# Strided and local attention with a hard-swish feed-forward on one core: where the first two batches' probabilities are turned, and how TensorE is kept busy before its first product

## The chip, the cores and the metric

The kernel runs on one core of a Trainium2 chip. A core has five instruction streams that matter here: TensorE (PE in the profile), VectorE (DVE), ScalarE (ACT), GpSimd (POOL), and SyncE (SP), which issues the DMAs. Each stream runs in its program order; a semaphore makes an instruction wait for another stream or a DMA. The metric is device microseconds from start to end, the median of several runs.

## The reference

Eight batches, eight heads, 576 positions of 64. In heads 0 to 3 a query sees itself and the 31 positions before it; in heads 4 to 7 it sees earlier positions whose number leaves the same rest by 32. The result, reordered to 4608 tokens of 512, goes through a feed-forward layer of width 2048. Weights are in float64, q, k and v in float32.

```python
scores = scale * np.matmul(q, k.transpose(0, 1, 3, 2))
rel = pos[:, None] - pos[None, :]
mask_local = (rel >= 0) & (rel < stride)                       # heads 0..3, stride 32
mask_strided = (rel >= 0) & (pos[None, :] % stride == pos[:, None] % stride)
attn = softmax(np.where(masks, scores, -1e9)); x = attn @ v    # x: [4608, 512]
h = x @ w_in                                                   # w_in [512, 2048]
g = h * np.clip(h + 3.0, 0.0, 6.0) / 6.0
out = g @ w_out                                                # w_out [2048, 512]
```

## The kernel before

**One list of operations, one planner.** The kernel writes down all its work with `op(engine, cost, function, reads, writes, due)`. `Plan.emit` (line 93) then walks a clock of its own: at each step it takes the operation that can start first on some engine (of several, the one with the smallest due time), and the order so found becomes each engine's program order. An operation may name several engines with a cost for each; the planner then also picks the engine. Due times hang on `T0`, the planned start of the first feed-forward product, and on the start of each later tile. Costs and due times set only the order; on the chip semaphores set the times.

**Attention by pairs of heads.** A batch is four pairs, `pair(g)` (line 440), taken in the order of `TURNS` (0, 2, 1, 3 for batch 0); pairs 0 and 1 are local, 2 and 3 strided. A pair's steps: transposes of q and k (`qp`, `kp` on TensorE in batch 0), scores (`ps`), mask, maximum, `less` (subtract it), exponential, sum, reciprocal, `norm`; then the normalized scores `e` are turned and set out in a block matrix (`atstr` for strided pairs, `atloc` for local ones), one for each of the pair's two heads (j = 0 and 1); then the products with v (`pv`). Two score tiles, `e_130` and `e_228` in the listings, are shared by all pairs. In batches 0 and 1 `turn` does the turning and the setting out in one step: for each block of 32 rows one DVE transpose straight into its place (four of 32x256 for a strided head, line 684; six of 32x192 for a local one, line 687). From batch 2 on `flip` transposes the whole tile in place on DVE (line 690) and `spread` copies the blocks to their places on ACT (lines 697 and 700). The local pairs of batch 0 are turned on TensorE instead (`pe`, line 371).

**x in two parts.** In batches 0 and 1 `keep_x` (line 408) splits each `pv` into a rounded part (`hi`, ACT, line 426) and the rest (`lo`, DVE, line 429), because each product of the feed-forward layer is made of three TensorE products of parts: high by high, high by low, low by high (lines 856 to 858 for `ph`, 833 to 835 for `acc`). A pair has two halves, and both parts of both halves write the same two keys, so the planner puts them in one chain: hi, lo, hi, lo. The last 64 positions of a batch go to a `left` tile.

**Weights.** Float64 weights come in as pairs of integers (`rawi`, `rawo`), and five operations turn one block into two parts: two on ACT (lines 281 and 285), a join on DVE (line 289), the high part on ACT or POOL (lines 303 and 305), the low part on POOL (line 308).

**The first 60 us.** Before the first feed-forward product TensorE would stand still for stretches; where the planner's clock sees such a stretch (line 138) it fills in `idle` products of 128x384, one for each 0.64 us (line 1570), and ahead of the first of them 46 small ones. The first tile is `ffn(0)`; then come `ffn(1)`, `ffn(2)` and three tiles of two batches.

Of the kernel before, what the change touches and what calls it, by code (L numbers as in the profile page):

```python
# [31 lines left out]
AHEAD = 27.0  # L32
OPEN = 6.0
# [4 lines left out]
T0 = 44.0  # L38
# [18 lines left out]
FEW = 46  # L57


class Plan:  # L60
# [29 lines left out]
    def emit(self, idle):  # L90
# [21 lines left out]
        while done < len(ops):  # L112
# [61 lines left out]
def attention_ffn(ctx: ExitStack, tc, q, k, v, w_in, w_out, out):  # L174
# [230 lines left out]
    def x_keys(b, c):  # L405
        return [("x", b, c, i) for i in range(2)] if b < 2 else [raw_key(b, c)]

    def keep_x(nm, b, c, puts, due):
# [4 lines left out]
        for n, (bkey, what, place, size, rest) in enumerate(puts):  # L413
# [19 lines left out]
            op("ACT", 0.15 + size * (0.0019 if strided else 0.00085), hi, reads=[bkey] + (xk if rest else []), writes=kk, give=bkey if last and whole else None, due=due + n)  # L433
            if not whole:
                op("DVE", 0.15 + size * (0.002 if strided else 0.00105), lo, reads=[bkey], writes=kk, give=bkey if last else None, due=due + 0.2 + n)
# [4 lines left out]
    def pair(g):  # L440
# [237 lines left out]
        for j in range(2):  # L678
# [9 lines left out]
            if b >= 2:  # L688
# [16 lines left out]
                op("ACT", 6 * 0.31 if loc else 4 * 0.36, spread, reads=[ekeys[j]], writes=[akeys[j]], due=due - 1.9 + j)  # L705
# [31 lines left out]
        op("PE", 1.25 * slow, values, reads=[*akeys, *vkeys], writes=[*vb, *xk, lk], take=vb, due=due - 1001,  # L737
# [80 lines left out]
    def ffn(b):  # L818
        s0, puts = start[b], []
        chunk = TILE / NFC  # L820
        xk = {c: x_keys(b, c) if b < 2 else [("x", 1, c, i) for i in range(2)] for c in range(NCC)}

# [19 lines left out]
        def first_product(fc):  # L842
# [3 lines left out]
            for n_, c in enumerate(TURNS[b]):  # L846
# [12 lines left out]
                op("PE", 0.683, mm1, reads=xk[c] + wkeys, writes=[pk],  # L859
# [744 lines left out]
```

## Time and profile before

| | |
|---|---|
| median of 3 runs | 870.25 us (869.94 to 876.99) |
| the profiled execution's own time | 871.98 us |
| its span, first to last instruction | 870.2 us |
| mean granted TensorE clock | 0.993 |
| busy: PE / DVE / ACT / POOL | 847.4 / 539.0 / 558.9 / 616.6 us |
| TensorE instructions (matmuls) | 6962 |

The span is what the profile's rows add up to; the 1.8 us beside it lie outside the first and last instruction. The profiled execution took 1.7 us more than the median of the runs. A row of the timeline gives start, length, engine, line, names and the count of merged instructions, and in brackets the idle time ahead of it with what ended it; `issue` means that nothing in the profile ended it. A 128x512 row of TensorE is drawn with its whole length, but such products start some 0.23 us apart.

### The profile page before, as it was taken

How to read it: one execution, taken by the hardware profiler on the slowest of the kernel's cores; microseconds unless marked ns; L12 is line 12 of the kernel's file. 1: busy time of each engine (PE TensorE's matmuls, PEld its weight loads, DVE VectorE, ACT ScalarE, POOL GpSimd, SP SyncE). 2: the span in 40 equal slices, each digit the busy share in tenths (PEclk: the TensorE clock that was granted, in tenths of full speed). 3: DMA queues.
4: the chain of work that ended last, by engine and by line, in shares of the span. 5: the costliest groups of instructions: out<-in, count | busy, mean ns of one | idle time of the engine just before them, and what ended most of it. 6: DMA issues, size and time to landing. Idle time of an engine off the chain costs nothing.

```text
span 870.2 us, 18946 instructions
## 1 busy us (share of the span) xinstructions
PE 847.4 (97%) x6962; PEld 683.8 (79%) x6962; DVE 539.0 (62%) x898; ACT 558.9 (64%) x1246; POOL 616.6 (71%) x606
## 2 busy tenths in 40 slices
PE   8889999999999999999999999999999999999996
PEld 6667777887888788888888878788888778888884
DVE  5688878344454538454546664466767888555586
ACT  3687657678778865877677965776744645454441
POOL 4688877587547799766676994465975987767673
PEclk9999999999999999999999999999999999999998
DMA  8968723898984455898999897877666667866636
GB/s 194 330 138 233 234 41 73 210 281 245 279 234 108 128 129 141 233 266 233 269 277 289 274 301 214 237 204 189 183 202 193 185 180 222 240 202 192 183 122 145
DMA packets 323308, 179.12 MB, mean 206 GB/s; under 512 B 182864, under 2 KB 300368, under 8 KB 323216
## 3 DMA queue, kind: packets, MB, share of 16 engines
q1 hardware_dynamic: 318564, 176.27, 71.5%
q10 hardware_dynamic: 4652, 1.64, 0.9%
q8 instruction: 55, 0.90, 0.4%
q14 instruction: 37, 0.30, 0.1%
HBM read 136.97 MB, written 40.89 MB: 204 GB/s over the span
## 4 chain that ended last, share of the span: by engine, by line
PE 82%; DMA 5%; POOL 5%; DVE 4%; ACT 2%; issue 1%; SPq 0%; POOLq 0%; DVEq 0%; ACTq 0%
PE P L1129 8%; PE P L1130 8%; PE P L1131 8%; PE cP L1452 5%; PE cP L1453 5%; PE cP L1454 5%; PE acc L833 5%; PE ph L856 5%; PE ph L857 4%; PE ph L858 4%; PE acc L835 4%; PE acc L834 4%; PE acc L1214 3%; PE acc L1215 3%; PE acc L1216 3%; PE pv L399 2%
## 5 line engine op out<-in xcount | busy, mean ns | idle before, releaser
L1470 DVE SCALAR_TENSOR_TENSOR C<-cP,C 128x512 f32<-128x512 f32 x96 | 65.7, 687 | 40.4 <-PE cP L1454 39.5
L794 POOL TENSOR_TENSOR gl<-u,gh 128x512 fp32r<-128x512 f32 x48 | 65.2, 1361 | 33.3 <-ACT gh L790 17.1
L1141 DVE TENSOR_TENSOR G<-P,G 128x512 f32<-128x512 f32 x64 | 44.0, 689 | 65.6 <-PE P L1131 53.2
L1129 PE MATMUL P<-B_T,wr 128*128 128x512 f32 x192 | 76.1, 396 | 3.9 <-ACT G L1136 2.3
L833 PE MATMUL acc<-wo,gh 128*128 128x512 f32 x192 | 77.2, 402 | 0.0
L835 PE MATMUL acc<-wo,gl 128*128 128x512 f32 x192 | 75.2, 392 | 0.3 <-POOL gl L794 0.2
L834 PE MATMUL acc<-wo,gh 128*128 128x512 f32 x192 | 74.9, 390 | 0.0
L1130 PE MATMUL P<-B_T,wr 128*128 128x512 f32 x192 | 74.8, 390 | 0.0
L1131 PE MATMUL P<-B_T,wr 128*128 128x512 f32 x192 | 74.8, 390 | 0.0
L1136 ACT COPY G<-P 128x512 f32<-128x512 f32 x64 | 37.6, 587 | 52.2 <-PE P L1131 51.7
L1367 POOL TENSOR_TENSOR sp<-G,sp 128x512 fp32r<-128x512 f32 x34 | 47.6, 1411 | 24.6 <-ACT sp L1363 22.5
L665 POOL TENSOR_TENSOR e<-e,st 128x144 f32<-128x144 f32 (+1 forms) x64 | 44.9, 704 | 20.7 <-DVE st L661 15.2
L779 DVE SCALAR_TENSOR_TENSOR u<-u,ph 128x512 f32<-128x512 f32 x48 | 32.8, 684 | 38.0 <-ACT u L776 37.8
L856 PE MATMUL ph<-x,wi 128*128 128x512 f32 x128 | 52.5, 410 | 2.3 <-ACT x L426 1.2
L857 PE MATMUL ph<-x,wi 128*128 128x512 f32 x128 | 50.8, 397 | 1.4 <-DVE x L429 0.8
L700 ACT COPY atloc<-e 32x192 f32<-32x192 f32 x144 | 50.8, 353 | 1.9 <-DVE e L690 0.3
L776 ACT ACTIVATE u<-ph,three 128x512 f32<-128x512 f32 x48 | 33.0, 687 | 28.1 <-PE ph L858 27.8
L858 PE MATMUL ph<-x,wi 128*128 128x512 f32 x128 | 50.8, 397 | 0.0
L644 DVE TENSOR_REDUCE st<-e 128x8 f32<-128x144 f32 (+1 forms) x64 | 25.6, 412 | 35.8 <-POOL e L640 35.6
L1129 PE MATMUL P<-B_B,wr 128*128 128x512 f32 x120 | 47.1, 392 | 0.0
L1130 PE MATMUL P<-B_B,wr 128*128 128x512 f32 x120 | 46.8, 390 | 0.0
L1129 PEld LDWEIGHTS P<-B_T,wr 128*128 128x128 f32 x192 | 36.0, 188 | 13.7 <-ACT G L1136 3.6
(604 smaller groups left out, 2672.6 us busy)
## 6 DMA issues: line engine op xcount, KB each, us to landing
wr<-dA SPq DMA_DIRECT2D x72, 256.0 KB
or<-do SPq DMA_DIRECT2D x32, 512.0 KB
wr<-dSu SPq DMA_DIRECT2D x48, 256.0 KB
wr<-dSv SPq DMA_DIRECT2D x48, 256.0 KB
or<-do SPq DMA_DIRECT2D x48, 256.0 KB
rawi<-in_moe_w_in_dram SPq DMA_DIRECT2D x16, 512.0 KB
rawo<-in_moe_w_out_dram SPq DMA_DIRECT2D x16, 512.0 KB
do<-wo SPq DMA_DIRECT2D x16, 512.0 KB
```

Source lines behind the costliest of these rows:

```text
L700: nc.scalar.copy(at[PAD * (a + h):PAD * (a + h) + PAD, :, rows], e[rows, :, PAD * h:PAD * h + PAD])
L794: (nc.vector if tail else nc.gpsimd).tensor_tensor(out=to, in0=src(), in1=tiles[gk[0]].bitcast(F32), op=ALU.subtract)
L833: nc.tensor.matmul(acc, gh, woh, start=fc == 0, stop=False)
L834: nc.tensor.matmul(acc, gh, wol, start=False, stop=False)
L835: nc.tensor.matmul(acc, gl, woh, start=False, stop=end)
L856: nc.tensor.matmul(ph, wih, xh, start=n_ == 0, stop=False)
L857: nc.tensor.matmul(ph, wih, xl, start=False, stop=False)
L858: nc.tensor.matmul(ph, wil, xh, start=False, stop=n_ == NCC - 1)
L1129: nc.tensor.matmul(ph, wh, xh, start=fresh and k == 0, stop=False, skip_group_check=not fresh)
L1130: nc.tensor.matmul(ph, wh, xl, start=False, stop=False, skip_group_check=not fresh)
L1131: nc.tensor.matmul(ph, wl, xh, start=False, stop=k == 1, skip_group_check=not fresh)
L1470: nc.vector.scalar_tensor_tensor(out=tiles[ck], in0=tiles[bank], scalar=1.0 / 6.0, in1=tiles[ck], op0=ALU.mult, op1=ALU.add)
```

## The change

Five edits. (1) `emit` counts the first stretch of idle time from 2.6 us (`BEGIN`) and not from 0. (2) In batches 0 and 1 all pairs but the local ones of batch 0 use `flip` in place of `turn`; each block copy is an operation of its own that ACT, POOL or DVE may take. For that the zeroing of `atstr` and `atloc` gets a second key, and `values` reads a key for each block. Strided heads also get a small memset on POOL (`again`). (3) In `keep_x` the parts of a half have keys of their own: a half's lo waits for its own hi, and the second half's hi no longer waits for the first half's lo; the products read all these keys. (4) The copies to `left` get a due time 3 us later. (5) `T0` goes from 44 to 43, by which all due times move.

```diff
@@ Plan.emit
             if e == "PE" and t < WARM and t - free[e] > IDLE:
-                for i in range(int((t - free[e]) / IDLE)):
+                for i in range(int((t - max(free[e], BEGIN)) / IDLE)):
@@ constants
+FREE = 2
+LEFTS = 3.0
+BEGIN = 2.6
-T0 = 44.0
+T0 = 43.0
@@ zero
-        op(either(us), 0, go, writes=[key], due=due)
+        op(either(us), 0, go, writes=[key, ("zero",) + key], due=due)
@@ keep_x
-            kk = [lk] if rest else xk
+            kk = [lk] if rest else xk if whole else [("xh", b, c, n)] + ([] if n else xk)
-            op("ACT", ..., hi, reads=[bkey] + (xk if rest else []), writes=kk, ..., due=due + n)
+            op("ACT", ..., hi, reads=[bkey] + (xk if n or rest else []), writes=kk, ..., due=due + n + LEFTS * rest)
-                op("DVE", ..., lo, reads=[bkey], writes=kk, ...)
+                op("DVE", ..., lo, reads=[bkey, ("xh", b, c, n)], writes=[("xl", b, c, n)], ...)
@@ pair
-            if b >= 2:
+            if b >= 2 or b == 1 or b == 0 and not loc:
                 op("DVE", 0.55 if loc else 0.4, flip, writes=[ekeys[j]], due=due - 2 + j)
-                op("ACT", 6 * 0.31 if loc else 4 * 0.36, spread, reads=[ekeys[j]], writes=[akeys[j]], due=due - 1.9 + j)
+                if b < FREE:
+                    for a in range(n // PAD):
+                        for h in range(1 + loc):
+                            def set_out(e, a=a, h=h, j=j):
...
+                                if e == "ACT":
+                                    nc.scalar.copy(at, x)
+                                else:
+                                    on(e).tensor_copy(at, x)
+                            own = [(akeys[j], 2 * a + h)] if a + h else akeys[j:j + 1]
+                            op({"ACT": 0.33, "POOL": 0.42, "DVE": 0.37} if loc else {"ACT": 0.4, "POOL": 0.5, "DVE": 0.44}, 0, set_out,
+                               reads=[ekeys[j], ("zero",) + akeys[j]], writes=own, due=due - 1.9 + j)
+                else:
+                    op("ACT", ..., spread, reads=[ekeys[j]], writes=[akeys[j]], due=due - 1.9 + j)
@@ values, ffn: reads
+ [(x, i) for x in akeys for i in range(8) if b < FREE]
+ parts[c]        # the ("xh", ...) and ("xl", ...) keys of batch b, pair c
```

The planner makes a new order of all engines up to about the middle of the second-last tile (`P_5_3`); behind that, and on SP for the first 73 rows, the order is the same. On TensorE the first `idle` row goes from x7 to x3, and by the end of pair 1's products with v 12 matmuls fewer have been issued (each `idle` product is two).

Three places, in the listing of program order. First TensorE behind the scores of pair 3 (`ps_3`), before:

```order
L1570 MATMUL idle<-ident 128x384 x3
L371 MATMUL pe_10_801<-ident,e_130 64x96 x6
L856 MATMUL ph_0_814<-x_00_702,wi_790 128x512
L857 MATMUL ph_0_814<-x_01_703,wi_790 128x512
L858 MATMUL ph_0_814<-x_00_702,wi_790 128x512
L856 MATMUL ph_1_822<-x_00_702,wi_790 128x512
L857 MATMUL ph_1_822<-x_01_703,wi_790 128x512
L858 MATMUL ph_1_822<-x_00_702,wi_790 128x512
L371 MATMUL pe_11_830<-ident,e_228 64x96 x6
```

and of the change:

```order
L876 MATMUL ph_0_788<-x_00_698,wi_715 128x512
L877 MATMUL ph_0_788<-x_01_699,wi_715 128x512
L878 MATMUL ph_0_788<-x_00_698,wi_715 128x512
L876 MATMUL ph_1_804<-x_00_698,wi_715 128x512
L877 MATMUL ph_1_804<-x_01_699,wi_715 128x512
L878 MATMUL ph_1_804<-x_00_698,wi_715 128x512
L876 MATMUL ph_2_811<-x_00_698,wi_715 128x512
L877 MATMUL ph_2_811<-x_01_699,wi_715 128x512
L878 MATMUL ph_2_811<-x_00_698,wi_715 128x512
L374 MATMUL pe_10_817<-ident,e_130 64x96 x6
```

The three idle products are gone, and nine of pair 0's products stand ahead of the transposes of pair 1.

Second, DVE from pair 1's x (`x_11`) to the first low part of pair 3's x (`x_31`), before; `fi` and `fo` rows are joins of weight blocks:

```order
L429 TENSOR_TENSOR x_11_913<-pv_10_859,x_10_912 128x288
L684 STREAM_TRANSPOSE atstr_269<-e_130 32x8x32 x4
L429 TENSOR_TENSOR x_11_913<-pv_11_860,x_10_912 128x224
L684 STREAM_TRANSPOSE atstr_272<-e_228 32x8x32 x4
L289 SCALAR_TENSOR_TENSOR fo_937<-fo_937,rawo_514 128x512
L289 SCALAR_TENSOR_TENSOR fo_940<-fo_940,rawo_518 128x512
L289 SCALAR_TENSOR_TENSOR fo_960<-fo_960,rawo_523 128x512
L429 TENSOR_TENSOR x_31_992<-pv_30_962,x_30_991 128x4x4x16
```

and of the change:

```order
L432 TENSOR_TENSOR x_11_902<-pv_10_850,x_10_901 128x288
L719 COPY atstr_266<-e_130 32x8x32
L292 SCALAR_TENSOR_TENSOR fi_891<-fi_891,rawi_355 128x512
L661 TENSOR_REDUCE st_3_799<-e_228 128x8
L432 TENSOR_TENSOR x_11_902<-pv_11_851,x_10_901 128x224
L664 RECIPROCAL st_3_799<-st_3_799 128x8
L292 SCALAR_TENSOR_TENSOR fo_895<-fo_895,rawo_502 128x512
L292 SCALAR_TENSOR_TENSOR fo_930<-fo_930,rawo_510 128x512
L693 STREAM_TRANSPOSE e_228<-e_228 128x256
L292 SCALAR_TENSOR_TENSOR fo_936<-fo_936,rawo_514 128x512
L292 SCALAR_TENSOR_TENSOR fo_988<-fo_988,rawo_519 128x512
L432 TENSOR_TENSOR x_31_994<-pv_30_970,x_30_993 128x4x4x16
```

Eight transposes became a flip for each head (the first, of `e_130`, stands just ahead of these rows) and one of the block copies; the other copies are on POOL and ACT.

Third, POOL from the second weight block's low part to the norm of pair 3's second head and what follows it, before:

```order
L308 TENSOR_TENSOR wi_838<-fi_689,wi_838 128x512
L308 TENSOR_TENSOR wi_840<-fi_727,wi_840 128x512
L1537 MEMSET vloc 32x128
L665 TENSOR_TENSOR e_130<-e_130,st_3_785 128x8x18
L665 TENSOR_TENSOR e_228<-e_228,st_3_785 128x8x18
L308 TENSOR_TENSOR wi_917<-fi_828,wi_917 128x512
L308 TENSOR_TENSOR wo_924<-fo_902,wo_924 128x512
```

and of the change:

```order
L668 TENSOR_TENSOR e_130<-e_130,st_3_799 128x8x18
L1557 MEMSET vloc 32x128
L651 TENSOR_TENSOR e_228<-e_228,st_3_799 128x8x18
L719 COPY atstr_266<-e_130 32x8x32 x3
L706 MEMSET e_130 128x8
L308 CAST wi_932<-fi_891 128x512
L311 TENSOR_TENSOR wi_932<-fi_891,wi_932 128x512
L668 TENSOR_TENSOR e_228<-e_228,st_3_799 128x8x18
L311 TENSOR_TENSOR wo_948<-fo_895,wo_948 128x512
L719 COPY atstr_268<-e_228 32x8x32 x2
```

Between the norms of pair 3's two heads POOL now has three block copies, a memset, and the two steps of the fourth weight block; two more copies follow behind another weight step.

More of the change, by code (lines that the diff above doesn't have):

```diff
@@ L429, in lo @@
                 nc.vector.tensor_tensor(out=to(1), in0=what(tiles[bkey.key]), in1=to(0).bitcast(F32), op=ALU.subtract)
-            kk = [lk] if rest else xk
             last = all(x[0] is not bkey for x in puts[n + 1:])
             whole = rest or b >= 2
-            op("ACT", 0.15 + size * (0.0019 if strided else 0.00085), hi, reads=[bkey] + (xk if rest else []), writes=kk, give=bkey if last and whole else None, due=due + n)
+            kk = [lk] if rest else xk if whole else [("xh", b, c, n)] + ([] if n else xk)
+            op("ACT", 0.15 + size * (0.0019 if strided else 0.00085), hi, reads=[bkey] + (xk if n or rest else []), writes=kk, give=bkey if last and whole else None, due=due + n + LEFTS * rest)
             if not whole:
-                op("DVE", 0.15 + size * (0.002 if strided else 0.00105), lo, reads=[bkey], writes=kk, give=bkey if last else None, due=due + 0.2 + n)
+                op("DVE", 0.15 + size * (0.002 if strided else 0.00105), lo, reads=[bkey, ("xh", b, c, n)], writes=[("xl", b, c, n)], give=bkey if last else None, due=due + 0.2 + n)
     def pair(g):
@@ L704, in pair @@
                 op("DVE", 0.55 if loc else 0.4, flip, writes=[ekeys[j]], due=due - 2 + j)
-                op("ACT", 6 * 0.31 if loc else 4 * 0.36, spread, reads=[ekeys[j]], writes=[akeys[j]], due=due - 1.9 + j)
+                if b < FREE:
+                    for a in range(n // PAD):
+                        for h in range(1 + loc):
+                            def set_out(e, a=a, h=h, j=j):
+                                rows = slice(PAD * a, PAD * a + PAD)
+                                x, at = e_whole(j)[rows], tiles[akeys[j]]
+                                x = x[:, :, PAD * h:PAD * h + PAD] if loc else x
+                                at = at[PAD * (a + h):PAD * (a + h) + PAD, :, rows]
+                                if e == "ACT":
[6 more added lines that the diff above has]
+                else:
+                    op("ACT", 6 * 0.31 if loc else 4 * 0.36, spread, reads=[ekeys[j]], writes=[akeys[j]], due=due - 1.9 + j)
                 if not loc:
@@ L736, in values @@
                                      ats[j][:, i].rearrange("p (a m) -> p a m", a=4)[:, :, :NPOS], start=True, stop=True)
-        op("PE", 1.25 * slow, values, reads=[*akeys, *vkeys], writes=[*vb, *xk, lk], take=vb, due=due - 1001,
+        op("PE", 1.25 * slow, values, reads=[*akeys, *vkeys] + [(x, i) for x in akeys for i in range(8) if b < FREE], writes=[*vb, *xk, lk], take=vb, due=due - 1001,
            room=0.0 if early else ROOM, mode="v")
@@ L821, in ffn @@
         xk = {c: x_keys(b, c) if b < 2 else [("x", 1, c, i) for i in range(2)] for c in range(NCC)}
+        parts = {c: [(x, b, c, n) for x in ("xh", "xl") for n in range(3)] if b < 2 else [] for c in range(NCC)}
         def mm2(fc, gk):
@@ L858, in mm1 @@
                     nc.tensor.matmul(ph, wil, xh, start=False, stop=n_ == NCC - 1)
-                op("PE", 0.683, mm1, reads=xk[c] + wkeys, writes=[pk],
+                op("PE", 0.683, mm1, reads=xk[c] + parts[c] + wkeys, writes=[pk],
                    due=s0 + (fc + n_ * 0.12) * chunk, mode="f")
```

## The prediction

> **What bounds the kernel now.** I read the table of windows first, to see where TensorE stands still at all. Its columns are the window, its length, then each engine's busy time (with its count), the granted clock, the DMA share and GB/s.
>
> ```profile
> 0.00:60.00 60.00, 51.18 (x927) 38.93 (x928) 41.03 (x92) 36.44 (x81) 36.02 (x60) 0.94 0.84 231
> 60.00:100.00 40.00, 39.45 (x407) 30.76 (x405) 34.78 (x65) 29.30 (x53) 36.17 (x32) 1.00 0.75 213
> 100.00:140.00 40.00, 39.18 (x389) 31.34 (x386) 29.68 (x60) 23.66 (x44) 32.06 (x31) 1.00 0.38 85
> 140.00:500.00 360.00, 360.00 (x3312) 291.41 (x3311) 189.32 (x349) 271.81 (x691) 260.48 (x291) 1.00 0.79 220
> ```
>
> TensorE is the bound: from 140 to 500 us it is busy all the time. The change works in batches 0 and 1, that is in the first 140 us, where TensorE stands still for 8.8, 0.6 and 0.8 us. From the tile `P_5_3` on, the order is the old one. So what the change wins or loses is the shift with which the dense stream of products goes on at 140 us, and a shift carries to the end, since TensorE sets the end.
>
> Within the first 60 us I then asked for TensorE's waits (line, what ended the wait, us, times, longest). The two longest have no releaser:
>
> ```profile
> PE ps L600 <- issue: 2.5, 2, 1.3
> PE pe L371 <- issue: 2.1, 1, 2.1
> ```
>
> The timeline of TensorE shows what they are:
>
> ```profile
> 18.16 1.02 PE L600 MATMUL ps<-kplain,qplain 64*64 64x36 f32 x55 [1.34 <-issue]
> 19.10 1.22 PE L371 MATMUL qp<-ident,qn 72*64 72x72 f32 x32
> 20.25 0.91 PE L1570 MATMUL idle<-ident 128*128 128x384 f32 x2
> 21.10 1.22 PE L371 MATMUL kp<-ident,kn 72*64 72x72 f32 x32
> 22.15 0.58 PE L371 MATMUL pe<-ident,e 96*64 96x96 f32 x5
> 24.83 2.14 PE L371 MATMUL pe<-ident,e 96*64 96x96 f32 x19 [2.10 <-issue]
> ...
> 35.55 0.42 PE L600 MATMUL ps<-kt,qt 64*64 64x36 f32 x11 [1.13 <-issue]
> ```
>
> Count the matmuls from one stop to the next: 55 + 32 + 2 + 32 + 5 = 126, each with a weight load. A stop in the middle of a group of equal products, after a fixed number of instructions, is TensorE out of instructions. In the DMA view of 22.4 to 24.8 us, which is the wait ahead of 24.83, one packet of the instruction queue came in, among 233 of data:
>
> ```profile
> q8 instruction: 1, 0.02, 2.8%
> ```
>
> [...]
>
> The last waits before the dense stream are for pair 3's x, the high part of the first row, then the low part:
>
> ```profile
> 53.76 0.50 PE L856 MATMUL ph<-x,wi 128*128 128x512 f32 x1 [1.20 <-ACT x L426]
> 54.76 0.50 PE L857 MATMUL ph<-x,wi 128*128 128x512 f32 x1 [0.49 <-DVE x L429]
> ```
>
> So two things end last at the start: the fetching of TensorE's instructions up to 35.55 us, and pair 3's way from its scores to 54.76 us.
>
> **Part 1: four idle products fewer.** The first stretch of them and what follows:
>
> ```profile
> 2.79 5.58 PE L1570 MATMUL idle<-ident 128*128 128x384 f32 x14
> 8.30 1.21 PE L371 MATMUL qp<-ident,qn 96*64 96x96 f32 x24
> ```
>
> Fourteen matmuls are seven products, 5.5 us to the next work, and the last of them lie 0.32 us apart (5.58 less the slow first ones and the last one's end); eight matmuls fewer let `qp` start about 8 x 0.32 = 2.6 us sooner, at 5.7. If the data of q are not there by then, it is less. [...] The DMAs on SP stand in the old order, and none of the first 36 waits for a product of TensorE that moves. So I expect the stops to end where they ended, near 18.2, 24.8 and 35.6 us, with longer waits ahead of them. Bounds: 0 when all is lost, 2.6 us when none is. I take **-0.3 us**, nearer to 0, because the row at 35.55 shows the stops still in force just before the feed-forward products. With 12 matmuls fewer ahead of it, TensorE stands 12 instructions further on in its program at each later stop; after 35.55 this only matters if pair 3 is earlier too.
>
> **Part 2: pair 3's way in batch 0.** Removed are transposes on DVE; what the flip and the copies cost is seen in later batches, which have them already (busy us, mean ns of one):
>
> ```profile
> L684 DVE STREAM_TRANSPOSE atstr<-e 32x256 f32<-32x256 f32 x32 | 13.9, 434 | 2.3 <-POOL e L665 2.0
> ...
> L690 DVE STREAM_TRANSPOSE e<-e 128x256 f32<-128x256 f32 x24 | 10.4, 439 | 9.2 <-POOL e L665 9.2
> ```
> ```profile
> L697 ACT COPY atstr<-e 32x256 f32<-32x256 f32 x96 | 38.6, 402 | 8.7 <-DVE e L690 7.8
> ```
>
> A head's four transposes, 4 x 0.434 = 1.74 us, become a flip of 0.44: DVE loses 1.3 us for each of four strided heads. In return there are 16 copies: by the listing 9 on POOL, 5 on ACT, 2 on DVE. A copy on POOL is not in this trace. Its bounds are 0.2 us (less than half of ACT's 0.402) and 0.85 us (POOL's cast of twice the size, below); I take 0.5, between ACT's copy and POOL's operations of 144 columns, 0.45 to 0.64.
>
> The relief on DVE shows first in the first weight block, whose join stood behind pair 2's transposes, and whose low part was POOL's until 39.05:
>
> ```profile
> 33.78 1.20 DVE L289 SCALAR_TENSOR_TENSOR fi<-fi,rawi 128x512 int32<-128x512 int32 x1
> ```
> ```profile
> 37.78 1.27 POOL L308 TENSOR_TENSOR wi<-fi,wi 128x512 fp32r<-128x512 f32 x1
> ```
>
> In the new order this join stands behind a flip, not four transposes (1.3 us), and ahead of two low parts, a sum and a reciprocal (some 1.2 us by their shapes): it runs from 31.3 to 32.5, and POOL does the cast and the low part (0.85 + 1.39) by 34.7 in place of 39.05. Pair 0's products can then start right behind the stop of 35.55, and not behind that low part at 39. That is 3 us in hand. Now POOL's rows up to pair 3's second norm (the group table, up to 140 us):
>
> ```profile
> L308 POOL TENSOR_TENSOR wi<-fi,wi 128x512 fp32r<-128x512 f32 x16 | 22.2, 1394 | 1.7 <-ACT wi L303 1.3
> L794 POOL TENSOR_TENSOR gl<-u,gh 128x512 fp32r<-128x512 f32 x14 | 19.3, 1386 | 5.1 <-ACT gh L790 2.6 <-issue 2.2 <-PE ph L857 0.3
> L308 POOL TENSOR_TENSOR wo<-fo,wo 128x512 fp32r<-128x512 f32 x14 | 19.1, 1367 | 0.7 <-ACT wo L303 0.5
> L665 POOL TENSOR_TENSOR e<-e,st 96x384 f32<-96x384 f32 x8 | 8.5, 1059 | 1.8 <-DVE st L661 1.8
> L648 POOL TENSOR_TENSOR e<-e,st 96x384 f32<-96x384 f32 x8 | 7.6, 951 | 10.9 <-DVE st L644 7.9 <-PE pv L735 2.9
> L305 POOL CAST wi<-fi 128x512 fp32r<-128x512 f32 x8 | 6.8, 852 | 3.2 <-DVE fi L289 3.2
> L665 POOL TENSOR_TENSOR e<-e,st 128x144 f32<-128x144 f32 x8 | 5.0, 635 | 4.9 <-DVE st L661 4.9
> L305 POOL CAST wo<-fo 128x512 fp32r<-128x512 f32 x6 | 4.8, 796 | 2.1 <-DVE fo L289 2.1
> L648 POOL TENSOR_TENSOR e<-e,st 128x144 f32<-128x144 f32 x8 | 3.7, 475 | 0.6 <-DVE st L644 0.6
> L640 POOL TENSOR_TENSOR e<-e,mtri 128x144 f32<-128x144 f32 x4 | 1.8, 450 | 2.3 <-ACT e L626 2.3
> ```
>
> Between that low part and the second norm of pair 3 the new order has on POOL: two norms of pair 1 (2.12), three casts (2.56) and three low parts of weight blocks (4.18), two masks (0.90), two subtractions (0.95) and two norms of pair 3 (1.27), three block copies (1.5) and two small memsets (0.3): 13.8 us. From 34.7 this is 48.5. Then follow on POOL a weight's low part (1.37; the flip, 0.44, runs beside it) and two copies (1.0), at 50.9; ACT's two copies are done by then. From the products with v to the first product with the low part it took 54.76 - 50.45 = 4.3 us before:
>
> ```profile
> 50.45 1.22 PE L735 MATMUL pv<-atstr,v 128*64 128x72 f32 x32
> ```
>
> The same way leads now to **55.2**, where it was 54.76. DVE is relieved, but the work went to POOL, which stands in the same way. Half a us is within what such a chain can tell; I take **0 us**. Bounds: five copies at 0.2 give -1.5, at 0.85 +1.8, and the start of the chain is good to 1 us: -2.5 to +2.8. The parts of x side by side save at most the second half's wait for the first half's low part, 0.6 us, which lies here beside a weight step that ACT has between the halves. The `left` copies 3 us later, and `T0`, cost nothing: an order of ACT, and due times that all move alike.
>
> **Part 3: batch 1.** TensorE's waits from 60 to 300 us are for the gate on DVE and 0.2 us for POOL:
>
> ```profile
> PE ph L856 <- DVE u L779: 1.1, 2, 0.8
> PE acc L835 <- POOL gl L794: 0.2, 1, 0.2
> ```
>
> DVE loses 1.3 us for each of four strided heads and somewhat more for each of four local ones, and gets 16 of the 40 copies at about 0.4: 5 us less in all. POOL gets 12 copies, some 6 us, into windows in which it is busy for 36.17 and 32.06 of 40 us. The waits for DVE should go, a new one for POOL may come. I take **-1.0 us**, from -1.3 (all gone) to +1.5 (a wait of a low part's length behind copies on POOL).
>
> **Sum.** -0.3 + 0 - 1.0 = -1.3 us. Against the profiled execution: span 870.2 to 868.9, its own time 871.98 to 870.7. That execution lay 1.7 us over the median of the runs; against the median, 870.25, the change gives **868.9 us**.
>
> **Rivals.**
>
> *Slower, by the clock.* Half clock follows windows of 3.41 us in which TensorE was busy for half the time:
>
> ```profile
> 52.23:55.64 3.41, 1.72 (x7) 0.94 (x6) 2.47 (x4) 2.76 (x8) 3.41 (x3) 1.00 0.73 173
> 55.64:59.05 3.41, 3.41 (x10) 2.67 (x9) 1.86 (x3) 2.47 (x5) 2.81 (x3) 0.50 0.21 36
> ```
>
> A window at 0.50 lets 8 to 10 products start where 15 fit, and costs 1.1 to 1.6 us. In the new order pair 0 to 2's products are done sooner, and TensorE waits for pair 3 in one long piece, by part 2 some 3 us ahead of the products with v and 2 us behind them. With two windows under 1.7 us busy in place of one, one more half-speed window falls on the dense stream: +1.4, and with copies on POOL at 0.85 us +1.8: 870.25 - 1.3 + 3.2 = **872.1**. It decides when the wait for pair 3 is over 3.4 us in all. [...]
>
> *Faster, the shift goes through.* If the stops at instruction blocks shrink when TensorE comes sooner, the 2.6 us of part 1 arrive, pair 3's scores come sooner, and POOL's copies are cheap: -2.6 - 1.0 = **866.6**. [...] Against it stands that three stops of over 1 us are in the rows above.
>
> *Nothing moves.* The stops hold, pair 3 is POOL's, and batch 1's DVE waits become POOL waits: **870.2**. For it: POOL's 36.17 of 40.
>
> **How the numbers follow.** Forecast (868.9, from 867.5 to 869.7) 0.40; nothing moves (to 871) 0.20; slower by the clock 0.20; faster 0.18; the rest 0.02. The range takes in the bounds of part 2 and the rivals, without their ends: 865.0 to 872.6. Faster or slower by over 1%, about what a measurement of this kernel can tell from no change, would be under 861.5 or over 879.0: no sum above comes near, so 0.03 each and 0.94 within.
>
> **What the new profile would show.** Part 1: first `qp` at 5.7, and stops without a releaser ending near 18.2, 24.8 and 35.6 us. Part 2: pair 0's products right behind the stop of 35.6; POOL without idle time from 35 to 49; the first product with pair 3's low part near 55.2. Part 3: no wait for line 798 (the gate) of over 0.5 us from 80 to 140 us. Wrong if the stops end sooner by over 1 us, if pair 3's low part is there before 53, or if a second window at 0.50 stands between 50 and 62.

## The result, and the profile after

The changed kernel is slower: **877.59 us** in the median of 8 runs (873.54 to 878.33), against 871.36 us for the kernel before in runs beside it; ratio 1.0065, 95% interval 1.0046 to 1.0084. Forecast were 868.9 us and a range up to 872.6, so it lies 5 us over the range: 6.2 us more than the kernel before, where 1.3 us less was forecast. The profiled execution took 878.33 us (span 876.2).

The table of windows of the changed kernel, to be read against the rows of before (window, length, busy time with counts of TensorE, its weight loads, VectorE, ScalarE and GpSimd, granted clock, DMA share, GB/s):

```profile
0.00:60.00 60.00, 52.21 (x910) 40.40 (x911) 34.65 (x81) 35.25 (x82) 40.61 (x74) 0.81 0.81 231
60.00:100.00 40.00, 37.11 (x371) 28.56 (x370) 35.01 (x54) 29.25 (x56) 35.09 (x39) 0.98 0.73 209
100.00:140.00 40.00, 38.46 (x406) 30.80 (x404) 29.69 (x55) 26.59 (x52) 33.58 (x38) 1.00 0.38 84
```

TensorE stands still for 2.9 us from 60 to 100 (0.6 before) and for 1.5 from 100 to 140 (0.8 before), and its mean clock over the first 60 us is 0.81 in place of 0.94. VectorE, which was to get 5 us less in batch 1, is as busy as it was: 35.0 and 29.7 us against 34.8 and 29.7.

I matched TensorE's program in the two traces by the count of products done, idle products left out. The changed kernel is 2.2 us ahead just before pair 3's products, 1.8 us behind when the dense stream runs at full clock (62 us), some 5.5 behind near 150 us and 6.3 behind at the end. What TensorE waits for between 60 and 300 us is VectorE's gate (line, what ended the wait, us in all, times, longest); it was 1.1 us before:

```profile
PE ph L876 <- DVE u L798: 5.5, 5, 1.5
```

The rows for the start, from TensorE's timeline, are the first `qp`, the one stop that is left, pair 3's products with v, and its first products with the high and the low part of x:

```profile
6.80 1.21 PE L374 MATMUL qp<-ident,qn 96*64 96x96 f32 x24
...
17.64 1.51 PE L603 MATMUL ps<-kplain,qplain 64*64 64x36 f32 x47 [2.21 <-issue]
...
52.03 1.22 PE L754 MATMUL pv<-atstr,v 128*64 128x72 f32 x30 [2.71 <-POOL atstr L719]
54.77 0.79 PE L876 MATMUL ph<-x,wi 128*128 128x512 f32 x1 [1.52 <-ACT left L429]
55.45 0.80 PE L877 MATMUL ph<-x,wi 128*128 128x512 f32 x1
```

Pair 3's low part came at 55.45; 55.2 was forecast. The two waits ahead of it, 2.71 and 1.52 us, were followed by half clock in two windows, where there was one before (third column TensorE's busy time, 0.50 and 0.67 the clock; the windows are not cut where the clock changed, it stood at half from 54.4 to 61.2 us):

```profile
48.79:52.20 3.41, 0.70 (x8) 0.36 (x8) 1.76 (x2) 1.77 (x5) 3.23 (x6) 1.00 0.69 134
52.20:55.61 3.41, 1.89 (x32) 1.35 (x30) 2.05 (x4) 3.28 (x9) 3.41 (x4) 0.82 0.78 153
55.61:59.02 3.41, 3.41 (x8) 2.66 (x9) 1.69 (x3) 1.97 (x4) 3.25 (x4) 0.50 0.00 0
59.02:62.43 3.41, 3.41 (x12) 2.70 (x11) 2.81 (x4) 3.16 (x6) 2.26 (x3) 0.67 0.00 0
```

For batch 1, the table of groups from 60 to 140 us gives what a block copy costs on each engine (busy us, mean ns of one):

```profile
L719 DVE COPY atstr<-e 32x256 f32<-32x256 f32 x9 | 6.4, 708 | 0.2
L719 DVE COPY atloc<-e 32x192 f32<-32x192 f32 x7 | 4.6, 663 | 0.1
L719 POOL COPY atloc<-e 32x192 f32<-32x192 f32 x9 | 3.4, 380 | 3.1 <-DVE e L693 1.7 <-ACT u L795 1.1
```

A copy on VectorE took 0.7 us where a transpose took 0.43 and 0.37; 16 of them are 11.0 us, and with the eight flips (4.0 us) VectorE has 15.0 us of work where 40 transposes were 15.8. Yet a copy can be short, as this row at 44.59 us of VectorE's timeline shows:

```profile
44.59 0.28 DVE L719 COPY atstr<-e 32x256 f32<-32x256 f32 x1
```

And this is the longest stretch ahead of a late gate, first on VectorE, then on GpSimd:

```profile
87.78 5.59 DVE L292 SCALAR_TENSOR_TENSOR fi<-fi,rawi 128x512 int32<-128x512 int32 x2
93.29 0.67 DVE L798 SCALAR_TENSOR_TENSOR u<-u,ph 128x512 f32<-128x512 f32 x1
```
```profile
86.99 1.31 POOL L311 TENSOR_TENSOR wo<-fo,wo 128x512 fp32r<-128x512 f32 x1
88.27 1.28 POOL L813 TENSOR_TENSOR gl<-u,gh 128x512 fp32r<-128x512 f32 x1
89.51 1.60 POOL L668 TENSOR_TENSOR e<-e,st 96x384 f32<-96x384 f32 x2
91.08 1.74 POOL L311 TENSOR_TENSOR wi<-fi,wi 128x512 fp32r<-128x512 f32 x1
```

Two joins of weight halves take 3.9 and 1.8 us here, where two others, at 81.8 and 82.4 us of the same timeline, took 0.68 each; and just here GpSimd works through five operations with two operands and no break. The first join ends 0.6 us after GpSimd's fourth operation, and GpSimd's fifth is stretched to 1.74 us (1.28 is the shortest of its form). The gate behind the joins is 1.2 us late for TensorE:

```profile
94.02 0.50 PE L876 MATMUL ph<-x,wi 128*128 128x512 f32 x1 [1.17 <-DVE u L798]
```

The chain that ended last goes through this place (start, us, what): it books 2.79 us of the first join as "issue", in which the engine waited for nothing that the profile shows.

```profile
88.80 2.79 issue
91.59 1.78 DVE fi L292
```

### The profile page after: what moved, and what is told of

The parts are those of the page before. It is cut to its first block, busy times and chain, and to the rows that moved or that the text cites. A ratio compares the mean times of both kernels' runs of the same rounds, so it can differ in the third digit from the quotient of the medians.

```text
span 876.2 us, 18970 instructions
## 1 busy us (share of the span) xinstructions
PE 850.8 (97%) x6950; PEld 686.9 (78%) x6950; DVE 534.7 (61%) x873; ACT 561.9 (64%) x1258; POOL 626.2 (71%) x639
## 4 chain that ended last, share of the span: by engine, by line
PE 78%; POOL 7%; DMA 5%; DVE 4%; ACT 2%; issue 2%; SPq 1%; POOLq 0%; DVEq 0%; ACTq 0%
PE P L1149 8%; PE P L1150 8%; PE P L1151 8%; PE cP L1472 5%; PE cP L1473 5%; PE cP L1474 5%; PE ph L876 4%; PE acc L853 4%; PE acc L855 4%; PE acc L854 4%; PE ph L877 4%; PE ph L878 4%; PE acc L1234 3%; PE acc L1236 3%; PE acc L1235 3%
## 5 line engine op out<-in xcount | busy, mean ns | idle before, releaser
L876 PE MATMUL ph<-x,wi 128*128 128x512 f32 x128 | 53.6, 418 | 7.0 <-DVE u L798 5.5
L668 POOL TENSOR_TENSOR e<-e,st 96x384 f32<-96x384 f32 (+1 forms) x64 | 44.6, 699 | 19.0 <-DVE st L664 18.5
L877 PE MATMUL ph<-x,wi 128*128 128x512 f32 x128 | 51.6, 403 | 0.0
L878 PE MATMUL ph<-x,wi 128*128 128x512 f32 x128 | 51.0, 399 | 0.0
L661 DVE TENSOR_REDUCE st<-e 96x6 f32<-96x390 f32 (+1 forms) x64 | 27.0, 425 | 34.3 <-ACT e L658 18.0
L1149 PE MATMUL P<-B_B,wr 128*128 128x512 f32 x120 | 47.7, 397 | 0.1
L693 DVE STREAM_TRANSPOSE e<-e 128x256 f32<-128x256 f32 (+1 forms) x60 | 29.9, 500 | 28.6 <-POOL e L668 28.3
L1150 PE MATMUL P<-B_B,wr 128*128 128x512 f32 x120 | 46.9, 391 | 0.0
L1151 PE MATMUL P<-B_B,wr 128*128 128x512 f32 x120 | 46.8, 390 | 0.0
```

What stands on the lines that cost most here:

```text
L876: nc.tensor.matmul(ph, wih, xh, start=n_ == 0, stop=False)
L877: nc.tensor.matmul(ph, wih, xl, start=False, stop=False)
L878: nc.tensor.matmul(ph, wil, xh, start=False, stop=n_ == NCC - 1)
L1149: nc.tensor.matmul(ph, wh, xh, start=fresh and k == 0, stop=False, skip_group_check=not fresh)
L1150: nc.tensor.matmul(ph, wh, xl, start=False, stop=False, skip_group_check=not fresh)
L1151: nc.tensor.matmul(ph, wl, xh, start=False, stop=k == 1, skip_group_check=not fresh)
```

## The experiments

Ratios are to the kernel before, in runs beside each kernel. "Waits" are TensorE's waits from 60 to 300 us for VectorE's gate, in the profiled execution.

| run | median us | ratio (95%) | waits |
|---|---|---|---|
| changed kernel | 877.59 | 1.0065 (1.0046-1.0084) | 5.5 |
| e1: VectorE's copies as transposes | 879.35 | 1.0084 (1.0052-1.0116) | 3.5 |
| e2: before, fewer idle products | 870.68 | 0.9997 (0.9982-1.0011) | 1.1 |
| e3: batch 1 as before | 874.51 | 1.0045 (1.0023-1.0068) | 1.5 |
| e4: batch 0 as before | 874.29 | 1.0035 (1.0018-1.0053) | 2.3 |
| e5: batch 1's copies on ScalarE | 882.31 | 1.0120 (1.0092-1.0149) | 7.5 |
| e6: before, copies for transposes | 878.87 | 1.0095 (1.0069-1.0122) | 5.0 |
| e7: idle products ahead of pair 3 | 877.13 | 1.0061 (1.0038-1.0083) | 6.0 |
| e8: batch 0 without GpSimd | 882.89 | 1.0143 (1.0114-1.0171) | 4.4 |
| e9: planner's costs as measured | 880.09 | 1.0104 (1.0076-1.0131) | 0.7 |
| e10: batch 1's copies as transposes | 879.31 | 1.0096 (1.0069-1.0123) | 6.7 |
| e11: batch 0's copies as transposes | 879.15 | 1.0084 (1.0055-1.0113) | 6.0 |
| e12: small edits undone | 878.27 | 1.0076 (1.0053-1.0098) | 0.2 |
| e13: joins as transposes | 868.24 | 0.9968 (0.9950-0.9987) | 2.0 |
| e14: before, joins as transposes | 868.54 | 0.9961 (0.9946-0.9976) | 0.8 |
| e15: gates first | 878.16 | 1.0082 (1.0067-1.0097) | 4.6 |
| e16: before, gates first | 871.32 | 1.0001 (0.9987-1.0014) | 1.1 |
| e17: joins, two operands, no wait for ScalarE | 878.97 | 1.0075 (1.0045-1.0104) | 5.8 |

**Which part costs what (e2, e3, e4).** e2 is the kernel before with the new first row of idle products alone; e3 and e4 are the changed kernel with one batch put back on `turn`.

```diff
 e2, in the kernel before:
-                for i in range(int((t - free[e]) / IDLE)):
+                for i in range(int((t - max(free[e], BEGIN)) / IDLE)):
 e3, in the changed kernel:
-            if b >= 2 or b == 1 or b == 0 and not loc:
+            if b >= 2 or b == 0 and not loc:
 e4, in the changed kernel:
-            if b >= 2 or b == 1 or b == 0 and not loc:
+            if b >= 2 or b == 1:
```

> The kernel before with 4 idle products fewer in the first row (3 in place of 7) and no other change of order. Theory of the prediction (the stops of instruction fetching end at the same times): 869 to 871, the change to the kernel before between 0 and -0.6 us. Theory C (the clock): the stop near 18 us leaves TensorE busy for under 1.7 us of a window of 3.41 us, the clock stands at half from 18 to over 28 us, and the start is no sooner: 870.5 to 872.5. If the shift goes through: 868.

> The changed kernel with batch 1 on the old transposes of VectorE; batch 0 and the first idle row as changed. Theory A: TensorE's waits for VectorE's gate from 60 to 300 us go from 5.5 back to 1 to 2 us, what is lost by 62 us (some 1.8 us) stays: 872 to 874. Theory B, or the later start alone being the cause of batch 1's waits: 876 or more.

> The changed kernel with batch 0 on the old transposes of VectorE; batch 1 and the first idle row as changed. If batch 0's loss (pair 3's copies behind GpSimd's low parts, some 1.8 us) and batch 1's (some 4.5 us) are separate terms: 875 to 876.5. If batch 1's waits are only a consequence of the late start: 871 to 873.

The idle products are worth nothing that can be measured: -0.2 us between the medians, with an interval of -1.6 to +1.0. e2's one trace would have said otherwise: it runs 1.9 us ahead of the kernel before at pair 3's products with v (48.60 against 50.45) and 1.5 us ahead from 100 us on. Single executions scatter by more than what is sought here. From e2, batch 0's change adds 3.8 us (e3 less e2), batch 1's 3.6 us (e4 less e2), and the changed kernel has 6.9 us over e2: the two losses stand side by side and nearly add up, as far as differences that are each good to 2 or 2.5 us can tell. So batch 1's waits are no mere consequence of the late start. In e3 and e4 the planner made a new order, though: e3 has the changed kernel's order for the first 60 us; e4's is neither that of the changed kernel nor that of the kernel before, the first 60 us included. The shares are those of whole plans, not of the copies alone.

**Is it the copies? (e1, e10, e5, e11, e6).** These keep the planned order and change only what an instruction is, or which engine issues it at the planned place.

```diff
 e1:  -  on(e).tensor_copy(at, x)
      +  (nc.vector.transpose if e == "DVE" else on(e).tensor_copy)(at, x)
 e10: +  (nc.vector.transpose if b == 1 else on(e).tensor_copy)(at, x)
 e11: +  (nc.vector.transpose if b == 0 else on(e).tensor_copy)(at, x)
 e5:  -  if e == "ACT":
      +  if e == "ACT" or b == 1:
 e6, in turn() of the kernel before, both transposes:
      -  nc.vector.transpose(
      +  (nc.vector.tensor_copy if b == 1 else nc.vector.transpose)(
```

> The changed kernel with every engine's order untouched; only the 18 block copies that VectorE got (2 in batch 0, 16 in batch 1) are issued as transposes of the same blocks, so that the values in these blocks lie turned and batch 0's and 1's output is not the reference's. Theory A (VectorE and GpSimd get in each other's way: a copy on VectorE, 0.28 us when alone, took 0.65 on average and up to 1.38 beside GpSimd, while a transpose takes 0.43 beside GpSimd or not): VectorE's 18 operations fall from 11.7 to some 7.4 us, TensorE's waits for the gate of VectorE between 60 and 300 us fall from 5.5 to 1 to 2.5 us, and the time from 877.6 to 873.5 to 875.5. Theory B (the waits come from where the planner put the rows, not from how long the copies take): the waits stay at 5 us or more, and the time stays within 1 us of the changed kernel's.

> The kernel before, order untouched, with batch 1's 40 block transposes on VectorE issued as copies of the same blocks (the blocks then lie unturned, so that batch 1's output is not the reference's). If a copy on VectorE waits for GpSimd and a transpose does not: 40 operations go from 15.8 us (0.434 and 0.368 each) to 25 us or more, TensorE's waits for the gate between 60 and 165 us go from 1.1 to over 3 us, and the time from 870.9 to 873 to 877. If a copy costs what a transpose costs (or less, 0.3 alone): 870 to 871.5.

e6 shows that a copy beside GpSimd is dear (groups from 60 to 140 us; the transposes were 434 and 368 ns):

```profile
L687 DVE COPY atloc<-e 32x192 f32<-32x192 f32 x17 | 14.7, 863 | 0.9 <-POOL e L665 0.7
L684 DVE COPY atstr<-e 32x256 f32<-32x256 f32 x16 | 8.9, 554 | 1.0 <-POOL e L665 0.9
```

The waits rose to 5.0 us and the median by 7.5 us, with no row moved. In the changed kernel the 18 copies on VectorE took 0.25 to 1.38 us: seven ran beside no operation of GpSimd or only beside its block copies, and took 0.25 to 0.39 (the one of 0.28 at 44.59 stood beside two of these copies); one beside a cast took 0.46, and the ten that overlap one of GpSimd's operations with two operands took 0.43 to 1.38. The transposes of strided blocks in the kernel before took 0.43 to 0.44 us on average both with GpSimd busy all the while and with GpSimd idle (15 of them each way). But theory A fell in e1: there the 16 copies of batch 1 took 430 and 370 ns as transposes, the waits went down to 3.5 us and the stall at 78 us vanished, and the median did not fall. The two joins took 3.9 and 1.8 us still, and new waits for GpSimd came up, 0.9 us for a weight's low part and 0.4 us for that of a gated product.

> The changed kernel, order untouched, with batch 1's 28 copies of VectorE and GpSimd all issued on VectorE as transposes of the blocks (batch 1's output is then not the reference's): VectorE has 4 us of flips and some 11 us of transposes, about what it had before, GpSimd has no copies, ScalarE keeps 12. If the work of the copies on GpSimd and the waits of VectorE's copies for it are the loss of batch 1: waits for the gate and for GpSimd between 60 and 300 us of 1 to 2.5 us (5.5 in the changed kernel, 3.9 with VectorE's copies alone issued as transposes), and 873.5 to 875. If the new plan's places are the loss: waits of 4 us or more and 877 or more.

> The changed kernel with the order of TensorE and SyncE untouched; the 28 block copies of batch 1 that VectorE (16) and GpSimd (12) got are issued by ScalarE at the places where the planner had them. The run with transposes in place of VectorE's copies left waits of 3.5 us for the gate and a new one of 0.9 us for a weight's low part on GpSimd. Theory A2 (it is the load on VectorE and GpSimd together: either one relieved alone leaves the other late): the waits of batch 1 for VectorE and GpSimd fall from some 5.5 to under 2 us and the time to 873 to 875. Theory B (the places of the joins, gates and low parts in the new plan): waits of 3.5 us or more for VectorE and GpSimd stay, and the time stays at 876 to 879. If ScalarE becomes late with its 15 us of copies, waits for it (x, u or gh) of over 1 us appear instead.

> The changed kernel, order untouched, with batch 0's 11 copies of VectorE and GpSimd all issued on VectorE as transposes of the blocks (output not the reference's in batch 0): GpSimd is rid of 4.3 us of copies before 52 us. If GpSimd's copies are what made pair 3 late: the wait of 2.7 us ahead of pair 3's products with v falls to 1.5 us or less, these start at 50 to 51 us in place of 52.0, one window of half clock or none follows, and the time is 874.5 to 876. If pair 3 is late by its place in GpSimd's order (a cast and a low part ahead of its last norm): still 51.5 or later, and 877 or more.

e10 gives VectorE the load that it had before and frees GpSimd of batch 1's copies, and keeps 6.7 us of waits: against theory A2. Its row on VectorE is that of the changed kernel again:

```profile
86.89 5.60 DVE L292 SCALAR_TENSOR_TENSOR fi<-fi,rawi 128x512 int32<-128x512 int32 x2
```

In e5, 36 copies on ScalarE (13.5 us by their groups) do not free VectorE either: 7.5 us. In e11 pair 3's products with v still waited 2.4 us, for blocks that VectorE turned behind a join of 1.4 us. So neither the copies' durations nor their engine explain the loss by themselves; what all these runs share is the plan.

**Clock, engines and small edits (e7, e8, e9, e12).** e7 puts four idle products ahead of pair 3's products with v. e8 takes GpSimd from batch 0's choice of engines, e9 sets the planner's costs, e12 puts `LEFTS` to 0, `T0` to 44 and the parts of x back under one key.

```diff
 e7, in values(), ahead of the products:
+            for i in range(4 if (b, c) == (0, 3) else 0):
+                nc.tensor.matmul(ps[0][:, :3 * P], tiles["ident",], tiles["ident",].unsqueeze(1).to_broadcast([P, 3, P]), start=True, stop=True)
 e8, batch 0:  -  {"ACT": 0.4, "POOL": 0.5, "DVE": 0.44}
               +  {"ACT": 0.4, "DVE": 0.44}
 e9, local:    +  {"ACT": 0.35, "POOL": 0.38, "DVE": 0.7}
     strided:  +  {"ACT": 0.4, "POOL": 0.45, "DVE": 0.7}
```

> The changed kernel with four idle products (2.6 us of TensorE at full clock) ahead of pair 3's products with v, where TensorE waited 2.7 us; nothing else is moved. Theory C (two waits in a row put the clock to half for 6.8 us when the dense stream starts, 54.4 to 61.1 us): the clock stays at 1.00 or is halved for one window at most, and the time falls by 1.5 to 3 us, to 874.5 to 876. If the clock is no part of the loss: 877.5 to 878.5.

> The changed kernel with batch 0's block copies allowed on ScalarE and VectorE alone (the plan is made anew). If pair 3's way was lost behind GpSimd (its two last copies started 0.8 us after the flip's end behind a low part of a weight, and took 0.6 each): pair 3's products with v come at or before 50.5 us, what is lost by 62 us falls from +1.8 to -1 us, and the time to 874 to 875.5, as with batch 0 as before. If it is lost by the norms on GpSimd, which the plan puts as late as before: 876.5 or more.

> The changed kernel with the planner's costs of a block copy put near what was measured: on VectorE 0.7 us in place of 0.44 and 0.37, on GpSimd 0.45 and 0.38, on ScalarE 0.40 and 0.35. The plan is made anew: 12 of the copies are VectorE's where 18 were. If the wrong cost led the planner to overload VectorE: waits for the gate between 60 and 300 us of under 3.5 us and 873 to 876. If the copies are too much for any engine, whoever gets them (24 us of work in batch 1 where the transposes took 15.8): 876 to 881.

> The changed kernel with its small edits undone together: the left copies at their old due time, T0 at 44, the two parts of x one after another under one key. The prediction gave them nothing, beyond at most 0.6 us that the parts of x could save. By it: 877 to 878.5. The plan is made anew, so what the sum of small shifts in the places does shows here too: more than 2 us to either side would be the plan's own doing.

e7's clock stayed at 1.00 from 46 to 64 us, and its median is 0.5 us lower than the changed kernel's, inside the intervals: the half clock is real, but what it costs can't be told from zero here, and it is not the bulk of what is lost. This kernel's runs go from 869.4 to 881.3. e8 had its wait for the copies gone (0.5 us for VectorE in place of 2.7 for GpSimd) and lost more elsewhere. In e9 the waits for the gate went down to 0.7 us, and TensorE waited 2.6 us for a weight's cast on GpSimd and 1.6 us for low parts instead. In e12 the waits in batch 1 went as well, and 3.5 us of waits for a reload of weights came from 519 us on. In each of the three the plan was made anew, and the loss came up at another place. Nothing speaks against the forecast that the small edits cost nothing, but with a new plan e12 doesn't show it either.

**The joins (e13, e14, e17, e15, e16).** The join of a weight's halves reads two operands in SBUF. e13 and e14 issue all 32 as a transpose of one tile, in the changed kernel and in the kernel before, every row in its place; e17 keeps two operands, but both the same tile.

```diff
 e13, e14, in join():
-            nc.vector.scalar_tensor_tensor(out=f, in0=f, scalar=3, in1=bits(),
-                                           op0=ALU.logical_shift_left, op1=ALU.bitwise_or)
+            nc.vector.transpose(f, f)
 e17:
+            nc.vector.scalar_tensor_tensor(out=f, in0=f, scalar=3, in1=f,
+                                           op0=ALU.logical_shift_left, op1=ALU.bitwise_or)
 e15, e16, in emit(): rows of the finished order
+        for x in [x for x in rows if self.tag.get(x[2]) == "gate"]:
+            i = rows.index(x)
+            j = max([k for k in range(i) if rows[k][3] == "DVE"], default=None)
+            if j is None or self.tag.get(rows[j][2]) != "join" or any(r[2] is not None and rows[j][2] in ops[r[2]][2] for r in rows[j:i]):
+                continue
+            rows.insert(i, rows.pop(j))
```

> The changed kernel, order untouched, with VectorE's 32 joins of weight halves issued as transposes of the same tile (one operand in place of two, the weights' low bits are left out and the blocks lie turned, so the output is not the reference's). Theory D (the new plan puts two joins ahead of a gate just where GpSimd starts 5.8 us of two-operand work without a break, and the joins wait for it): every join takes near 0.7 us, TensorE's waits for the gate between 60 and 300 us fall from 5.5 to under 3 us, and the time from 877.6 to 873 to 875. Theory B (other places of the plan): 876.5 or more.

> The same in the kernel before (32 joins as transposes, order untouched). The joins took 32.3 us there too, with one of 2.5 us ahead of a gate. Theory D: the waits of 1.1 us for the gate go, the time falls by 0.5 to 1.5 us to 869.5 to 870.5, and the difference between the two kernels with joins as transposes is 3 to 4.5 us (what batch 0 costs), not 6 to 7. Theory B: the difference stays at 6 us or more.

> The changed kernel, order untouched, with VectorE's 32 joins reading the same tile as both operands: two operands as before, but no wait for ScalarE's low halves, whose bits are left out of the weights (the output is not the reference's). Theory D (joins with two operands wait for GpSimd): joins of 3.9 and 1.8 us ahead of the gate at 93 us stay, waits for the gate of 4 us or more, 875 to 878.5. If it was the wait for ScalarE that the transposes removed: 868 to 870.

The whole loss is gone: 868.24 us for the changed plan, 868.54 for the old one. The same edit is worth 9.4 us in the one and 2.8 in the other. That is more than was expected of it: 873 to 875 us, and a difference of 3 to 4.5 us left over from batch 0. Nor is it the clock: over all runs the mean granted clock was 0.990 in e13, as in the changed kernel (0.993 in the kernel before). In e13 the joins take 0.69 each (groups of the whole span), and pair 3's products with v start at 48.53, 3.5 us sooner, behind a wait of 1.19 us in place of 2.71:

```profile
L292 DVE STREAM_TRANSPOSE fo<-fo 128x512 int32<-128x512 int32 x16 | 10.9, 688 | 2.6 <-ACT fo L284 2.5
L292 DVE STREAM_TRANSPOSE fi<-fi 128x512 int32<-128x512 int32 x16 | 10.8, 687 | 0.1
```
```profile
48.53 1.21 PE L754 MATMUL pv<-atstr,v 128*64 128x72 f32 x30 [1.19 <-POOL atstr L719]
```

Some 1.9 of these 3.5 us were there before, at 45 us, where e13's execution had spent 10.2 us at half clock and that of the changed kernel 17.1. The rest is GpSimd's: on pair 3's way it is GpSimd that waits for the joins. From its first block copy to its last it took 7.7 us in the changed kernel (44.28 to 51.98) and 6.1 in e13 (42.40 to 48.48), with the same operations in the same order. Two of them, a cast and a low part, first in the changed kernel, then in e13:

```profile
46.17 1.16 POOL L308 CAST wi<-fi 128x512 fp32r<-128x512 f32 x1
47.41 1.70 POOL L311 TENSOR_TENSOR wi<-fi,wi 128x512 fp32r<-128x512 f32 x1
```
```profile
43.93 0.61 POOL L308 CAST wi<-fi 128x512 fp32r<-128x512 f32 x1
44.62 1.31 POOL L311 TENSOR_TENSOR wi<-fi,wi 128x512 fp32r<-128x512 f32 x1
```

So the joins and GpSimd's operations hold each other up, and the edit takes away both delays.

e17 is the control, since the transposes also freed the joins from waiting for ScalarE's low halves: with two operands and without that wait the time is 878.97, and VectorE's timeline has the two joins unchanged:

```profile
89.94 5.60 DVE L292 SCALAR_TENSOR_TENSOR fi<-fi 128x512 int32<-128x512 int32 x2
95.46 0.68 DVE L798 SCALAR_TENSOR_TENSOR u<-u,ph 128x512 f32<-128x512 f32 x1
```

> The changed kernel with three rows of VectorE exchanged and nothing else: where a join stands right ahead of a gate of batch 0 or 1, the gate comes first. One of the three is the second join ahead of the gate at 93.3 us. Theory D: the wait of 1.3 us there falls to 0 to 0.3, the waits of 60 to 300 us from 5.5 to some 4 us, and the time by 1 to 1.5 us, to 876 to 876.7. If the next engine is late anyway (a weight's low part on GpSimd): 877 to 878.

> The kernel before with six rows of VectorE exchanged in the same way. Its waits for the gate were 1.1 us in all between 60 and 300 us: 869.5 to 870.9, the one version that could come out under both kernels, if only by what a comparison can barely tell.

One exchange cannot mend it. In e15 TensorE's wait of 1.2 us ahead of the gate's products at 94 us is gone, but at 96 us products wait 0.9 us for the low part of a gated product on GpSimd, and the median stays. In the kernel before, six exchanges change nothing. No version that computes the reference came out under the kernel before by more than its interval.

## Why the prediction was wrong, point by point

**Part 1, the idle products (-0.3): the size right, the way half right.** e2 measured -0.2. The first `qp` started at 6.80, not 5.7: the six idle matmuls that are left took 0.67 us each, not 0.32. In the kernel before such matmuls started 0.64 us apart up to 4.2 us and 0.32 apart from 4.7 on; here they were still 0.64 apart at 6.1. That the stops end at their old times, from which the -0.3 us follows, no run shows: one of 2.21 us ended at 17.64, and no other of over 1 us followed while TensorE ran at half clock, from 17 to 34 us. What the two traces show is a count and a queue. The first stop came behind 349 matmuls in both kernels, and in the kernel before 126, 127 and 127 lie between the stops that ended at 18.16, 24.83, 29.42 and 35.55 us; the instruction queue brought 55 packets (the instruction blocks of the faster rival), 0.90 MB in all, for 6962 matmuls with a weight load each, one for some 127, and one started 2.2 to 2.9 us ahead of the end of each of the four stops (15.3, 22.5, 27.0 and 33.4 us). At 29.9 us nothing was left of the gain, as forecast, but the half clock had taken it along with the stop, where the forecast had the stops alone: the size is luck.

**Part 2, pair 3 (0, bounds -2.5 to +2.8): mis-sized; +3.8 by e3 less e2, good to 2.3 us.** The working along GpSimd's rows was good in its times: the second norm started at 49.06 (48.5 forecast), the low part of x came at 55.45 (55.2). Part of that is luck: undisturbed copies, casts and low parts took less than their prices (0.39 to 0.42, 0.61 and 1.28 us, against 0.5, 0.85 and 1.39), and what GpSimd lost to the joins filled the difference. In the changed kernel's trace 1.8 us are lost by 62 us, inside the bounds: 0.7 because the low part comes at 55.45 and not at 54.76, the rest in the second stretch of half clock, which the sum left to a rival. What makes up the other 2 us of e3 less e2, if they are there, is open.

**Part 3, batch 1 (-1.0, bounds -1.3 to +1.5): this is the step that failed; +3.1 by the changed kernel less e3, +3.6 by e4 less e2, each good to 2 to 2.6 us by the table's intervals.** "5 us less in all" on VectorE was 0.8 us, since a copy there took 0.7 and not 0.4. And the waits for the gate, which were to go, went from 1.1 to 5.5 us. I priced every operation by a mean, added up each engine by itself and asked which engine has more to do; that VectorE and GpSimd can wait for each other stood nowhere in the sum. The price of a join is not its mean: the kernel before has these two on VectorE, 10 us apart, and I had quoted one of 1.20 us without asking why.

```profile
82.48 0.65 DVE L289 SCALAR_TENSOR_TENSOR fi<-fi,rawi 128x512 int32<-128x512 int32 x1
...
92.72 2.51 DVE L289 SCALAR_TENSOR_TENSOR fi<-fi,rawi 128x512 int32<-128x512 int32 x1
```

The sum of the 32 joins hardly changed, 32.0 us before and 31.5 after. What changed is where the long ones stand: ahead of a gate, while GpSimd has no break. The rows show this for the gate at 93.3 us. Ahead of the late gates at 78.5 and 135.5 us the longest rows are block copies (1.38 and 1.32 us). e13, in which the joins alone were changed, leaves two of the five waits (0.8 and 1.1 us) and is still 9.4 us faster.

**The rivals.** The slower one by half clock did occur, a second window at half speed on the dense stream, but e7, which took it away, gained nothing that can be told from zero. "Nothing moves", with POOL waits in place of VectorE's, was the nearest in spirit: GpSimd had its part in the cause, but through waits that the trace books as busy time, of VectorE's joins in batch 1 and of GpSimd's own operations in batch 0. No rival had that, nor its size.

**The signs.** First `qp` at 5.7: wrong. Stops near 18.2, 24.8, 35.6: the first only. GpSimd without idle time from 35 to 49: right. Low part near 55.2: right. No wait for line 798 over 0.5 us from 80 to 140: wrong, three of 0.9 to 1.5. A second window at 0.50 near 55 to 62 was named as a sign against the forecast, and it stood there.

**What stays open.** e13 frees all 32 joins at once, so the share of single joins is not known, nor how much of batch 0's 3.8 us and batch 1's 3.1 to 3.6 us each of them makes. Why the replanned kernels (e8, e9, e12) lose at other places was not followed up. Each kernel was traced in one execution only, so how far its start is typical is not known.

## What to carry to other kernels

Before an operation is priced by its mean, look at its shortest and longest row: here a VectorE operation that took 0.65 us in one place and 3.9 in another was waiting, and its busy time hid it. Ask of each VectorE operation whether it reads two SBUF operands or is a copy (the joins took 0.63 to 3.9 us here, the copies 0.25 to 1.38), and what GpSimd does at that moment, for either can be the one that waits: here GpSimd's cast went from 0.61 to 1.16 us as well. Where both engines are nearly full (35.0 and 35.1 of 40 us here), a new order of the same work can lose more than the edit can save: it lost 6.2 us, where 1.3 were to be saved. When a planner makes the order, an experiment that keeps the order and changes one kind of instruction tells more than one that lets the plan be made anew.

## What the runs showed of the hardware

A join on VectorE with two SBUF operands took up to 3.9 us beside GpSimd's two-operand operations, 0.63 at the least, and waited not for one operation alone: it started at 87.78 and ended at 91.67, and in that time GpSimd began three more operations that ran through, at 88.27, 89.51 and 90.30 (1.28, 0.82 and 0.82 us), and at 91.08 one that took 1.74. GpSimd waits too: a cast that took 0.61 us at 38.38, with VectorE idle, took 1.16 at 46.17, beside joins. No run here shows what holds the two up, nor why the one that waits is passed over three times.

The half clock came in pieces of 3.41 us, up to 864 us in the kernel before and 870 us in the changed kernel: one each from 24.9 and 55.6 us in the kernel before, five in a row from 16.9 and two from 54.4 in the changed kernel; in e2, from 14 to 64 us, two from 19.2 and one each from 29.4 and 53.3. So the grid of these pieces lies elsewhere from one trace to the next. In the kernel before, the windows with TensorE busy for 1.32 and 1.72 us (from 21.50 and 52.23) were followed by one at 0.50, those with 2.15 and 2.68 us (from 14.67 and 31.74) by one at 1.00. In the changed kernel, TensorE was busy in every window from 18.1 to 31.7 us and stayed at 0.50; the first and the last of the four windows:

```profile
18.10:21.51 3.41, 3.41 (x72) 3.19 (x69) 0.65 (x2) 2.21 (x8) 0.45 (x1) 0.50 0.99 378
...
28.33:31.74 3.41, 3.41 (x98) 2.87 (x87) 2.83 (x8) 2.06 (x4) 1.50 (x2) 0.50 0.87 261
```

This, and the stops of TensorE at the start that nothing in the profile ended, from 0.31 us (the kernel before, at 29.42) to 4.05 us (e11, at 39.30), differ between the traces. That they also make the runs of one kernel differ (869.4 to 881.3 us in e7) is likely, but no kernel was traced twice.
